# ScalarE issues the mixing weights during step A; table parts, stores and conversion work move later

## The chip, the cores and the metric

One core of a Trainium2 chip. The metric is the device time of one execution of the kernel in microseconds (us), median of the runs. The engines are named as the profile names them: PE (TensorE, matmuls; PEld are its weight loads), DVE (VectorE), ACT (ScalarE), POOL (GpSimd) and SP (SyncE, which here only issues DMAs). ACT and POOL can issue DMAs too; "ACTq", "SPq" mark such instructions in the rows.

## The reference

A Fourier transform along the sequence, a complex mixing of the 256 channels with a soft threshold, the inverse transform, and then a two-layer network with a leaky activation on every token:

```python
def _attn_ref(x, w_r, w_i, b_r, b_i):          # x: (4, 3008, 256)
    X = np.fft.rfft(x, axis=1)
    Yr = Xr @ w_r - Xi @ w_i + b_r
    Yi = Xr @ w_i + Xi @ w_r + b_i
    Yr = np.sign(Yr) * np.maximum(np.abs(Yr) - 0.01, 0.0)   # and Yi alike
    return np.fft.irfft(Yr + 1j * Yi, n=x.shape[1], axis=1)

def _moe_ref(x, w_in, w_out, alpha):           # x: (12032, 256), d_ff 2048
    h = x @ w_in
    g = np.maximum(h, 0.0) + alpha * np.minimum(h, 0.0)
    return g @ w_out
```

## The kernel before

**Staging.** The transform of length 3008 = 47 x 64 is done in steps for each of the four batch elements. Step A (`a_load`, `a_mm`, `a_evac`) multiplies groups of rows by a small table (`lf_s`); batch 0 keeps its result in SBUF (`a0_s`), batch 1 stores it to DRAM (`ad`) from tiles called `ast`. Step B (`b_load` or `b_half`, `b_mm`) gathers that result transposed into tiles `bt` and multiplies it by the table `rb_s`; the mixing (`m_mm`, `m_evac`) multiplies by `w_r` and `w_i` and applies the threshold; step C (`c_mm`, `c_evac`) multiplies by the table `cf_s` and stores to DRAM (`zd`); step D (`d_load`, `d_step`) loads that back (`zt`) and turns it into tokens. After it the network's two layers run over chunks of tokens (`l1_step` and `l2_step` over the first twelve, `s_l1` and `s_l2` over the rest), with the other batch elements' steps worked in between. This main part takes over nine tenths of the time.

**The start.** Everything that this change touches lies before the main part. Steps A of batch 0 and the first four groups of batch 1 come first (loop over `seq`), then a loop over `t` from 0 to 12: turn `t` runs `b_mm(t)`, `m_evac(t-2)`, `m_mm(t-1)`, `c_mm(t-3)` and `c_evac(t-4)`. Behind the loop a list `TAIL` ends step C, then has the ten remaining early groups of step A of batch 1 (entries `f`, function `a_fill`), and step D's first two loads (entry `d`). Then step D and the first layer begin.

**The conversion.** Beside these turns the network's weights, 16 raw pieces of 512 KB, are loaded (`conv_load`, line L265) and split into a high and a low part for the matmuls. A piece's operations are cut into packets, four to a piece, in which the end of one piece is worked together with the beginning of the next. `pump(n)` works the next n packets; the list `PT` says how many in each turn. On ACT the packets show as L278 (first look at a raw piece; it waits for that piece's load), L287 and L288; on DVE as L279, L280, L289, L293, L296; on POOL as L290, L297. When `pump` starts a piece it also lets `conv_fetch` issue loads so that two raw pieces are on their way. Pieces 0 to 7 can be loaded from the start; 8 to 15 only after turn 10 has set `conv_m[1] = FT`.

**What sets the order.** The order on each engine is the order of this code (`manual_schedule`). Each engine works its list strictly in order, and an instruction whose data or buffer isn't there holds all behind it. PSUM tiles of steps A to C come from a pool of three (`ps_f`, tag `f`): a matmul group of step A needs the tile that the group three before it has been evacuated from. The mixing's PSUM tiles come from a pool of two. DMAs of SP and ACT share eight completion counters, and a DMA waits until the earlier one on its counter has landed. The tile `Yc` has one buffer; the fourth `ast` tile of batch 1 lives in it first, so the first `m_evac` (ACT, L514) waits until the store of that tile has landed.

Of the kernel before, what the change touches and what calls it, by code (L numbers as in the profile page):

```python
# [21 lines left out]
NSLOT = 24  # L22
# [74 lines left out]
def fft_mix_moe(ctx, tc, x, w_r, w_i, b_r, b_i, w_in, w_out, alpha, la, rb, lc, rd, lf, cf, sel, out):  # L97
    nc = tc.nc
# [51 lines left out]
    rb_s = const.tile([128, NSLOT, 128], F32, tag="rb", name="rb_s")  # L150
# [57 lines left out]

    mix_w = []

    def load_mix(*tags):
        for w, tag in zip((w_r, w_i), tags):
            t = work.tile([128, CT, C], F32, tag=tag, name="wm_f", bufs=1 if tag[1] in "tc" else None)
            nc.sync.dma_start(out=t, in_=w.rearrange("(k p) f -> p k f", p=128))
            mix_w.append(t)

    def load_rb(n0, n1, at=0):
        nc.sync.dma_start(out=rb_s[:, n0:n1], in_=rb[:, n0 + at:n1 + at])

    def load_cf(n0, n1):  # L220
        nc.gpsimd.dma_start(out=cf_s[:, n0:n1], in_=cf[:, n0:n1])
# [35 lines left out]
    def conv_load():  # L257

        m, i = divmod(conv_m[0], 2)
        conv_m[0] += 1  # L260
        k = conv_m[0] % 3
        raw = cw_s[:, NSLOT + 8 * k:NSLOT + 8 * k + 8].rearrange("p (k n) f -> p k (n f)", k=2)
        raw = raw.rearrange("p k (n w) -> p k n w", w=2)
        src = w_out.bitcast(U32)[256 * m:256 * m + 256] if i else w_in.bitcast(U32)[:, 512 * m:512 * m + 512]
        nc.sync.dma_start(out=raw.rearrange("p k n w -> p k (n w)"), in_=src.rearrange("(k p) f -> p k f", p=128))  # L265
        conv_raw.append((raw, m, i))

    def conv_first(raw, m, i):
        h, m = divmod(m, FH // 2)
        hi, lo = (wo_h[h][:, 2 * m:2 * m + 2, w] if i else wi_h[h][:, w, :, 256 * m:256 * m + 256] for w in range(2))  # L270
        shape = list(hi.shape)
        wh, wl = raw[:, :, :, 1], raw.bitcast(U16)[:, :, :, 1]
        tags = [conv_tags[k][(conv_m[0] + len(conv_raw)) % 2] for k in ("v1", "ex", "lf")]
        v1, ex, lf = (work.tile(shape, t, tag=tag, name="conv", bufs=3 if tag == "bt" else None)
                      for t, tag in zip((U32, U32, F32), tags))
        conv_old.append((wh, wl, v1, ex, lf, hi, lo))
        return [
            lambda: A.activation(out=f(v1), in_=f(wh), func=AF.Abs),  # L278
            lambda: V.tensor_scalar(out=f(v1), in0=f(v1), scalar1=LEAST, scalar2=MOST, op0=ALU.max, op1=ALU.min),  # L279
            lambda: V.tensor_scalar(out=v1, in0=v1, scalar1=0x07FFFFFF, scalar2=3,  # L280
                                    op0=ALU.bitwise_and, op1=ALU.logical_shift_left)]

    def conv_second(wh, wl, v1, ex, lf, hi, lo):
        es = V if ES[(conv_m[0] - 3 + len(conv_raw)) % len(ES)] else G

        def parts():
            A.activation(out=hi, in_=f(v1), func=AF.Copy)  # L287
            A.activation(out=lf, in_=wl, func=AF.Copy, scale=2.0 ** -36)  # L288
            V.tensor_scalar(out=ex, in0=v1, scalar1=0xFF800000, scalar2=None, op0=ALU.bitwise_and)  # L289
            G.tensor_tensor(out=lf, in0=lf, in1=f(ex), op=ALU.mult)  # L290

        return [
            lambda: V.scalar_tensor_tensor(out=v1, in0=wh, scalar=0xC0000000, in1=v1,  # L293
                                           op0=ALU.bitwise_and, op1=ALU.bitwise_or),
            parts,
            lambda: es.tensor_tensor(out=f(v1), in0=f(v1), in1=f(hi), op=ALU.subtract),  # L296
            lambda: G.tensor_tensor(out=lo, in0=f(v1), in1=lf, op=ALU.add)]  # L297
# [12 lines left out]
    def conv_fetch():  # L310
        assert not conv_ops
        while len(conv_raw) < 2 and conv_m[0] < conv_m[1]:
            conv_load()

    def pump(n):

        while n > 0:
            if not conv_ops:
                conv_fetch()
                second = conv_second(*conv_old.pop()) if conv_old else []  # L320
                first = conv_first(*conv_raw.pop(0)) if conv_raw else []
                first, second = ([(op,) for op in ops] for ops in (first, second))
                if first and second:
                    conv_ops.extend([second[0] + first[0], first[1], second[1], second[2] + second[3] + first[2]])
                else:
                    conv_ops.extend(first + second)
                if not conv_ops:
                    return
            for op in conv_ops.pop(0):
                op()  # L330
            n -= 1
# [67 lines left out]
    def a_evac(b, g):  # L399
        ps = pa.pop((b, g))  # L400
        if b == 0:
            st = a0_s[:, g]
        else:
            tag = A1_TAGS[g] if b == 1 and g < len(A1_TAGS) else "zst"
            st = work.tile([NQ, 2, C], F32, tag=tag, name="ast", bufs={"bt": 3, "zst": 3, "Yt": 1, "Yc": 1}.get(tag))
        if b == 0 and g % 2:
            V.tensor_copy(out=st, in_=ps)
        else:
            A.activation(out=st, in_=ps, func=AF.Copy)
        if b:  # L410
            stores.append((ad[b][:, 2 * g:2 * g + 2], st))
# [179 lines left out]
    def d_load(b, g):  # L591
        assert len(zdone) >= NPAIR * (b + 1) and not any(o.tensor is zd[b][:].tensor for o, i in stores)
        t = work.tile([NQ, CH, C], F32, tag="zt", name="zt")
        nc.sync.dma_start(out=t, in_=zd[b][:, CH * g:CH * (g + 1)])
        zt[b, g] = t
# [388 lines left out]
    NG = R // 2  # L984
    EARLY = 4
    FILL = 14
    C0 = 2
    PT = [0, 1, 3, 3, 3, 3, 3, 3, 4, 4, 4, 4]
    TAIL = [['me', 1], ['ce', 3], ['cm', 2], ['cm', 1], ['ce', 2], ['ce', 1], ['d'], ['f', 4], ['e'], ['f', 6]]
    WARM = 6  # L990
    A1_TAGS = ("zst", "zst", "Yt", "Yc", "bt", "bt", "bt", "Xh", "Xl", "Xh", "Xl", "zst", "zst", "Yc")
# [3 lines left out]
    def keep_warm(n):  # L995
        ps = ps_f.tile([128, 512], F32, tag="f", name="ps_idle")
        for _ in range(n):
            PE.matmul(ps[:, 0:128], idle, idle, start=True, stop=True)

    with tc.manual_schedule():  # L1000
# [6 lines left out]
            a_load(0, g)  # L1007
        for g in range(EARLY // 2):
            a_load(1, g)
        load_rb(0, 4, NSLOT)  # L1010
        load_mix("Yh", "Yh")
        conv_tags.update(v1=("yh", "yl"), ex=("xh", "xh"), lf=("xl", "xl"))
        seq = [(0, g) for g in range(NG)] + [(1, g) for g in range(EARLY)]

        for n, (b, g) in enumerate(seq):
            a_mm(b, g)
            if n >= 1:
                a_evac(*seq[n - 1])
            if n == NG // 2:
                b_half(0, 0)  # L1020
                b_half(1, 0)
            if n == NG:
                b_half(0, 1)
                b_half(1, 1)
                b_load(0, 2)
                load_rb(4, 12)
                for _ in range(C0):
                    conv_load()
                bias_parts()
# [5 lines left out]
        def run(fn, q, *args):  # L1035
            if 0 <= q < NPAIR:
                fn(0, q, *args)
# [10 lines left out]
        for t in range(NPAIR + 1):  # L1048
            if t == 1:
                keep_warm(8)  # L1050
            run(b_mm, t)
            run(b_load, t + 3)
            run(c_evac, t - 4)
            run(b_evac, t)
            run(m_evac, t - 2)
            run(m_mm, t - 1, ps_h)
            run(b_evac2, t)
            run(c_mm, t - 3)
            if t < NPAIR:
                pump(PT[min(t, len(PT) - 1)])  # L1060
            if t in (2, 5):
                load_rb(2 * t + 8, 2 * t + 14)
            if t < 8 and t % 2 == 0:
                load_cf(3 * t, 3 * t + 6)
            if t == 1:
                put()
            if t == 6:
                load_tables()
            if 5 <= t < 10:
                a_load(1, t - 3)  # L1070
            if t == NPAIR - 1:
                load_rb(0, 4)
            if t == 10:
                half(1)
                conv_m[1] = FT
        for op, *args in TAIL:
            if op == "f":
                a_fill(*args)
            elif op == "d":

                drain()
                d_load(0, 0)
                d_load(0, 1)
                conv_fetch()
                conv_m[1] = conv_m[0]
                hold.extend(conv_raw)
                conv_raw.clear()
            elif op == "e":
                flush()
            elif op == "p":  # L1090
                pump(*args)
            else:
                {"me": m_evac, "cm": c_mm, "ce": c_evac}[op](0, NPAIR - args[0])
# [126 lines left out]
        for k in range(len(spairs) + SLAG):  # L1220
# [9 lines left out]
            if k >= SLAG:  # L1230
                n, t = spairs[k - SLAG]
# [43 lines left out]
```

## Time and profile before

| | |
|---|---|
| median of 3 runs | 1354.2 us (1352.36 to 1355.0) |
| the profiled execution's own time | 1353.91 us |
| its span, first to last instruction | 1352.1 us |
| granted TensorE clock, mean | 1.000 |
| busy share of the span | PE 99%, PEld 92%, DVE 77%, ACT 56%, POOL 27% |
| chain of waits that ended last, share of the span | PE 89%, DMA 3%, DVE 2%, ACT 2%, issue 2% |
| mean busy share of the DMA engines in the first seven of 40 slices | 0.9, 0.9, 0.7, 0.4, 0.2, 0.2, 0.3 |

A busy PE isn't a PE at its peak: the ends of matmuls are modelled, and a matmul that starts late behind a wait shows the wait in brackets. In the timelines a row reads: start, duration, engine, line, operation, out<-in, shape, how many; in brackets the idle time of that engine just before and what ended it. Start to start of equal matmuls is the better measure of PE's pace. A queue's row gives packets, MB and its share of the time of the 16 DMA engines; a row of DMA issues gives how many, KB each and the median time to landing. A row of a merged group covers its members from the first start to the last end.

### The profile page before, as it was taken

Reading aid. Unit: us, or ns where it says so; the run is one execution under the profiler, and the core shown is the slowest. Engines: PE = TensorE matmul, PEld = TensorE weight load, DVE = VectorE, ACT = ScalarE, POOL = GpSimd, SP = SyncE. Lnnn points to the kernel's source line nnn. Section 1 sums busy time; section 2 is a strip of 40 time slices with the busy share of each in tenths; the row PEclk is TensorE's granted clock in tenths of the full one; section 3 lists DMA queues with packets and bytes.
Section 4 is the critical chain, followed back from the end, with each engine's and each line's share of the span. In section 5 each row is a group of like instructions: output and inputs, shape, how many; then the busy total and the mean of one; then the engine's idle time right before and its main releaser. Section 6 shows DMA issues by size and latency. Waiting matters only on the chain.

```text
span 1352.1 us, 25037 instructions
## 1 busy us (share of the span) xinstructions
PE 1334.2 (99%) x9144; PEld 1248.6 (92%) x9144; DVE 1034.8 (77%) x1940; ACT 761.3 (56%) x1526; POOL 371.7 (27%) x398
## 2 busy tenths in 40 slices
PE   8989999999999999999999999999999999999998
PEld 4969999999999999999999999999999999999998
DVE  3766866776777777776768888888888888888885
ACT  3556655665565655545556555555565555555653
POOL 3754642221322232222212211212112111211122
PEclk9999999999999999999999999999999999999999
DMA  9974223342334312111110110111011101110001
GB/s 226 246 203 152 88 95 98 104 135 86 98 97 129 98 64 82 48 55 48 36 36 1 40 29 1 40 28 28 3 38 28 29 5 36 29 28 7 23 17 28
DMA packets 88278, 89.91 MB, mean 66 GB/s; under 512 B 42157, under 2 KB 70544, under 8 KB 88155
## 3 DMA queue, kind: packets, MB, share of 16 engines
q1 hardware_dynamic: 80116, 77.55, 20.2%
q0 software_dynamic: 4912, 7.76, 2.2%
q10 hardware_dynamic: 3127, 3.01, 0.7%
q8 instruction: 72, 1.18, 0.4%
q14 instruction: 51, 0.42, 0.1%
HBM read 50.76 MB, written 34.34 MB: 63 GB/s over the span
## 4 chain that ended last, share of the span: by engine, by line
PE 89%; DMA 3%; DVE 2%; ACT 2%; issue 2%; POOL 0%; SPq 0%; ACTq 0%; DVEq 0%; POOLq 0%
PE ps_h L804 24%; PE ps_h L699 13%; PE ps_m L501 6%; PE ps_o L905 6%; PE ps_o L906 6%; PE ps_o L904 6%; PE ps_d L630 4%; PE ps_o L738 3%; PE ps_o L737 3%; PE ps_o L736 3%; PE ps_b L438 2%; PE o_last L737 1%; PE o_last L738 1%; PE o_last L904 1%; PE o_last L736 1%
## 5 line engine op out<-in xcount | busy, mean ns | idle before, releaser
L804 PE MATMUL ps_h<-yh,w 128*128 128x512 f32 (+1 forms) x960 | 315.6, 389 | 0.0
L843 POOL TENSOR_TENSOR l<-t,h 128x512 fp32r<-128x512 f32 x98 | 127.1, 1297 | 496.5 <-ACT h L841 455.7
L804 PEld LDWEIGHTS ps_h<-yh,w 128*128 128x128 f32 x960 | 180.0, 188 | 33.2
L808 DVE SCALAR_TENSOR_TENSOR sq<-sq,beta_s,ps_h 128x512 f32<-128x512 f32 (+1 forms) x240 | 167.8, 732 | 54.5 <-ACT sq L807 53.7
L699 PE MATMUL ps_h<-yh,w 128*128 128x384 f32 (+1 forms) x704 | 207.0, 337 | 1.3 <-DVE q L706 1.3
L804 PE MATMUL ps_h<-yl,w 128*128 128x512 f32 (+1 forms) x480 | 186.2, 388 | 0.0
L706 DVE SCALAR_TENSOR_TENSOR q<-q,beta_s,ps_h 128x384 f32<-128x384 f32 (+1 forms) x192 | 115.1, 600 | 91.8 <-ACT q L705 90.9
L710 ACT ACTIVATE gh<-q 128x384 fp32r<-128x384 f32 (+1 forms) x192 | 99.1, 516 | 148.6 <-DVE q L706 145.6
L711 POOL TENSOR_TENSOR gl<-q,gh 128x384 fp32r<-128x384 f32 (+1 forms) x90 | 96.8, 1076 | 275.9 <-ACT gh L710 266.4
L823 ACT ACTIVATE dh<-sq 128x768 fp32r<-128x768 f32 x112 | 94.8, 846 | 117.8 <-DVE sq L808 75.9
L807 ACT ACTIVATE sq<-ps_h 128x512 f32<-128x512 f32 (+1 forms) x240 | 133.2, 586 | 26.8 <-PE ps_h L804 25.5
L699 PEld LDWEIGHTS ps_h<-yh,w 128*128 128x128 f32 x704 | 129.3, 189 | 4.4 <-DVE q L706 1.2
L705 ACT ACTIVATE q<-ps_h 128x384 f32<-128x384 f32 (+1 forms) x192 | 91.9, 479 | 61.3 <-PE ps_h L699 60.5
L841 ACT ACTIVATE h<-t 128x512 fp32r<-128x512 f32 x98 | 62.0, 633 | 105.5 <-DVE t L839 103.2
L699 PE MATMUL ps_h<-yl,w 128*128 128x384 f32 (+1 forms) x352 | 116.5, 331 | 0.0
L738 PE MATMUL ps_o<-w,gl 128*128 128x256 f32 x384 | 108.0, 281 | 0.6 <-POOL gl L711 0.6
L737 PE MATMUL ps_o<-w,gh 128*128 128x256 f32 x384 | 107.8, 281 | 0.0
L736 PE MATMUL ps_o<-w,gh 128*128 128x256 f32 x384 | 107.7, 280 | 0.0
L804 PEld LDWEIGHTS ps_h<-yl,w 128*128 128x128 f32 x480 | 90.5, 189 | 13.6
L838 DVE TENSOR_TENSOR dl<-sq,dh 128x768 fp32r<-128x768 f32 x98 | 93.4, 953 | 3.8 <-ACT dh L823 3.7
L906 PE MATMUL ps_o<-l,sw_a 128*128 128x256 f32 x294 | 82.0, 279 | 0.0
L904 PE MATMUL ps_o<-h,sw_a 128*128 128x256 f32 x294 | 81.9, 279 | 0.0
(215 smaller groups left out, 3610.4 us busy)
## 6 DMA issues: line engine op xcount, KB each, us to landing
zt<-zd SPq DMA_DIRECT2D x32, 384.0 KB
zd<-zst SPq DMA_DIRECT2D x37, 256.0 KB
ad<-ast SPq DMA_DIRECT2D x48, 192.0 KB
bt<-ad SPq DMA_DIRECT2D x72, 128.0 KB
xt<-in_x SPq DMA_DIRECT2D x21, 320.0 KB
out<-oT SPq DMA_DIRECT2D x152, 32.0 KB
cw_s<-in_moe_w_in SPq DMA_DIRECT2D x8, 512.0 KB
cw_s<-in_moe_w_out SPq DMA_DIRECT2D x8, 512.0 KB
```

What stands on the lines that cost most here:

```text
L699: PE.matmul(ps, wi_h[m // FH][:, w, ct, 128 * (m % FH):128 * (m % FH) + 128], a[:, ct, 0:n], start=(k == 0), stop=(k == 3 * CT - 1))
L706: V.scalar_tensor_tensor(out=q, in0=q, scalar=beta_s[:, m:m + 1], in1=ps, op0=ALU.mult, op1=ALU.add)
L710: A.activation(out=hi, in_=q, func=AF.Copy)
L736: PE.matmul(a, hi[:, t], w[:, 0], start=(i, k) in first, stop=False)
L737: PE.matmul(a, hi[:, t], w[:, 1], start=False, stop=False)
L738: PE.matmul(a, lo[:, t], w[:, 0], start=False, stop=(i, k) in last)
L804: PE.matmul(ps, wi_h[m // FH][:, w, ct, 128 * (m % FH):128 * (m % FH) + 128], a[:, ct, 0:w1], start=(k == 0), stop=(k == 3 * CT - 1))
L807: A.activation(out=q[:, j], in_=ps, func=AF.Relu, scale=-1.0)
L808: V.scalar_tensor_tensor(out=q[:, j], in0=q[:, j], scalar=beta_s[:, m:m + 1], in1=ps, op0=ALU.mult, op1=ALU.add)
L843: G.tensor_tensor(out=l24, in0=t24, in1=f(h24), op=ALU.subtract)
L904: PE.matmul(o, wh, gh, start=first, stop=False)
L906: PE.matmul(o, wh, gl, start=False, stop=last)
```

## The change

Five edits:

- The three transfers of the mixing stage (`rb_s` table parts 0 to 3, `w_r`, `w_i`) are issued by ACT in the eighth turn of step A's loop (between ACT's fourth and fifth evacuation), not by SP behind all of step A's row loads.
- `C0`: one raw piece, not two, is loaded ahead of the loop over `t`; the next is then issued by `pump` in turn 1.
- `put()`, the four stores of batch 1's `ast` tiles, is called in turn 3, not turn 1; the table part `rb` 12 to 17 in turn 3, not 2; the parts of `cf` in turns 0, 3, 6, 8, not 0, 2, 4, 6.
- `PT`: turns 8 to 11 work three packets each, not four (31 in all before `TAIL`, 35 before).
- The four packets left over are worked in `TAIL`'s entry `d`, behind the issue of step D's two loads.

```diff
-    def load_mix(*tags):
+    def load_mix(*tags, queue=nc.sync):
...
-            nc.sync.dma_start(out=t, in_=w.rearrange("(k p) f -> p k f", p=128))
+            queue.dma_start(out=t, in_=w.rearrange("(k p) f -> p k f", p=128))
...
-    def load_rb(n0, n1, at=0):
-        nc.sync.dma_start(out=rb_s[:, n0:n1], in_=rb[:, n0 + at:n1 + at])
+    def load_rb(n0, n1, at=0, queue=nc.sync):
+        queue.dma_start(out=rb_s[:, n0:n1], in_=rb[:, n0 + at:n1 + at])
...
-    C0 = 2
-    PT = [0, 1, 3, 3, 3, 3, 3, 3, 4, 4, 4, 4]
+    C0 = 1
+    PT = [0, 1, 3, 3, 3, 3, 3, 3, 3, 3, 3, 3]
...
-        load_rb(0, 4, NSLOT)
-        load_mix("Yh", "Yh")
...
+            if n == 7:
+                load_rb(0, 4, NSLOT, nc.scalar)
+                load_mix("Yh", "Yh", queue=nc.scalar)
...
-            if t in (2, 5):
-                load_rb(2 * t + 8, 2 * t + 14)
-            if t < 8 and t % 2 == 0:
-                load_cf(3 * t, 3 * t + 6)
-            if t == 1:
+            if t in (3, 5):
+                load_rb(3 * t + 3, 3 * t + 9)
+            if t in (0, 3, 6, 8):
+                load_cf((t + 1) // 3 * 6, (t + 1) // 3 * 6 + 6)
+            if t == 3:
                 put()
...
                 d_load(0, 0)
                 d_load(0, 1)
+                pump(4)
                 conv_fetch()
```

**ACT, from the end of step C to step D** (L580 and L584: evacuation and store of step C; L409: evacuation of a group of step A). Before:

```order
L514 ACTIVATE Yc<-ps_m,lam_s 128x512 x2
L580 ACTIVATE zst<-ps_c 128x512
L584 DMA zd_437<-zst 128x2x256
L580 ACTIVATE zst<-ps_c 128x512
L584 DMA zd_437<-zst 128x2x256
L409 ACTIVATE ast<-ps_a 96x512 x4
L287 ACTIVATE w_911<-conv 128x2x256
L288 ACTIVATE conv<-cw_s 128x512
L409 ACTIVATE ast<-ps_a 96x512 x6
```

Now:

```order
L514 ACTIVATE Yc<-ps_m,lam_s 128x512 x2
L580 ACTIVATE zst<-ps_c 128x512
L584 DMA zd_431<-zst 128x2x256
L580 ACTIVATE zst<-ps_c 128x512
L584 DMA zd_431<-zst 128x2x256
L278 ACTIVATE conv<-cw_s 128x512
L287 ACTIVATE w_258<-conv 128x2x256
L288 ACTIVATE conv<-cw_s 128x512
L409 ACTIVATE ast<-ps_a 96x512 x4
L287 ACTIVATE w_903<-conv 128x2x256
L288 ACTIVATE conv<-cw_s 128x512
L409 ACTIVATE ast<-ps_a 96x512 x6
```

Three conversion operations now stand ahead of the evacuations of step A's ten groups; the first of them, L278, reads raw piece 8.

**SP, the same place** (L265: raw pieces; L218: the `rb` table; L584: a store of step C; L594: step D's loads). Before, where the first two L265 are raw pieces 8 and 9 and the third is piece 10:

```order
L265 DMA cw_s<-in_moe_w_in 128x2x512
L265 DMA cw_s<-in_moe_w_out 128x2x512
L218 DMA rb_s<-tab_rb 128x512
L584 DMA zd_437<-zst 128x2x256
L594 DMA zt<-zd_437 96x1024 x2
L265 DMA cw_s<-in_moe_w_in 128x2x512
L594 DMA zt<-zd_437 96x1024
```

Now, where the three L265 are pieces 8, 9 and 10:

```order
L218 DMA rb_s<-tab_rb 128x512
L584 DMA zd_431<-zst 128x2x256
L594 DMA zt<-zd_431 96x1024 x2
L265 DMA cw_s<-in_moe_w_in 128x2x512
L265 DMA cw_s<-in_moe_w_out 128x2x512
L265 DMA cw_s<-in_moe_w_in 128x2x512
L594 DMA zt<-zd_431 96x1024
```

Raw pieces 8 and 9 have moved from ahead of step C's last store to behind step D's first two loads.

**SP, from step A's last loads to the fourth raw piece** (L214: mixing weights; L420: gathers of step A's result; L339: the four `ast` stores). Before:

```order
L218 DMA rb_s<-tab_rb 128x512
L214 DMA wm_f<-in_w_r 128x2x256
L214 DMA wm_f<-in_w_i 128x2x256
L420 DMA bt<-a_83 64x1x256 x4
L218 DMA rb_s<-tab_rb 128x1024
L265 DMA cw_s<-in_moe_w_in 128x2x512
L265 DMA cw_s<-in_moe_w_out 128x2x512
L339 DMA ad_159<-ast 96x512 x4
L265 DMA cw_s<-in_moe_w_in 128x2x512
L218 DMA rb_s<-tab_rb 128x768
L265 DMA cw_s<-in_moe_w_out 128x2x512
```

Now:

```order
L420 DMA bt<-a_83 64x1x256 x4
L218 DMA rb_s<-tab_rb 128x1024
L265 DMA cw_s<-in_moe_w_in 128x2x512
L265 DMA cw_s<-in_moe_w_out 128x2x512
L265 DMA cw_s<-in_moe_w_in 128x2x512
L218 DMA rb_s<-tab_rb 128x768
L339 DMA ad_159<-ast 96x512 x4
L265 DMA cw_s<-in_moe_w_out 128x2x512
```

The first three rows have gone to ACT, and the four stores stand behind a third raw piece and a table part that followed them.

## Rows read from the trace of the kernel before

**Rows 1.** Stretches: busy us (count) of PE, PEld, DVE, ACT, POOL; clock, DMA share, GB/s

```profile
44.82:69.14 24.32, 24.32 (x186) 23.48 (x185) 21.13 (x28) 14.64 (x25) 22.28 (x27) 1.00 0.99 244
69.14:74.50 5.36, 5.09 (x38) 4.74 (x37) 3.88 (x5) 1.69 (x3) 5.02 (x6) 1.00 1.05 215
74.50:81.43 6.93, 5.39 (x39) 4.88 (x37) 4.24 (x7) 3.83 (x7) 2.51 (x3) 1.00 0.89 265
81.43:95.57 14.14, 12.14 (x76) 10.04 (x75) 10.90 (x18) 8.29 (x15) 10.51 (x11) 1.00 0.54 164
```

**Rows 2.** Timeline of PE: step A's ten groups of batch 1, idle matmuls, step D

```profile
95.57 8.76 PE L392 MATMUL ps_a<-xt,lf_s 94*96 94x512 f32 x24
104.16 0.83 PE L998 MATMUL ps_idle<-idle 128*128 128x128 bf16 x12
104.83 2.87 PE L630 MATMUL ps_d<-rd_s,zt 96*128 96x94 f32 x24
```

**Rows 3.** Timeline of ACT over the same stretch

```profile
97.04 1.08 ACT L409 ACTIVATE ast<-ps_a 96x512 f32<-96x512 f32 x2 [0.67 <-PE ps_a L392]
...
99.75 0.62 ACT L287 ACTIVATE w<-conv 128x512 fp32r<-128x512 f32 x1
100.27 0.66 ACT L288 ACTIVATE conv<-cw_s 128x512 f32<-128x512 uint16 x1
100.84 1.59 ACT L409 ACTIVATE ast<-ps_a 96x512 f32<-96x512 f32 x3
```

**Rows 4.** Timeline of SP's queue over the same stretch

```profile
98.54 0.81 SPq L594 DMA_DIRECT2D zt<-zd  x2
99.40 0.42 SPq L265 DMA_DIRECT2D cw_s<-in_moe_w_in  x1
```

**Rows 5.** DMA between 98.5 and 105.0: GB/s in 40 equal slices, and the sum

```profile
GB/s 0 0 0 0 0 0 176 176 0 126 176 277 328 479 429 277 353 303 227 277 252 277 227 265 277 240 252 252 214 239 328 391 403 378 277 164 25 0 0 0
DMA packets 496, 1.31 MB, mean 202 GB/s; under 512 B 48, under 2 KB 48, under 8 KB 496
```

**Rows 6.** Waits of SP's queue, 92 to 112: total us, times, longest

```profile
SPq L594 <- DMA zt<-zd: 2.6, 1, 2.6
```

**Rows 7.** Timeline of PE, turns 10 to 12: first matmul of the mixing

```profile
77.10 0.50 PE L481 MATMUL ps_m<-bias_p,ones 128*128 128x512 f32 x1 [1.54 <-DVE Y L515]
...
82.97 0.50 PE L481 MATMUL ps_m<-bias_p,ones 128*128 128x512 f32 x1 [0.49 <-DVE Y L515]
...
88.32 0.50 PE L481 MATMUL ps_m<-bias_p,ones 128*128 128x512 f32 x1 [0.85 <-DVE Y L515]
```

**Rows 8.** Timeline of ACT in turn 9: raw piece 6

```profile
78.28 0.66 ACT L278 ACTIVATE conv<-cw_s 128x512 f32<-128x512 f32 x1 [1.96 <-DMA cw_s<-in_moe_w_in]
78.85 0.62 ACT L287 ACTIVATE w<-conv 128x512 fp32r<-128x512 f32 x1
```

**Rows 9.** Timelines of SP, PE and ACT in the first turns, by engine

```profile
17.68 0.37 SPq L214 DMA_DIRECT2D wm_f<-in_w_i  x1
...
25.60 0.68 PE L438 MATMUL ps_b<-rb_s,bt 128*128 128x128 f32 x4 [1.12 <-DMA bt<-a]
27.84 0.68 PE L438 MATMUL ps_b<-rb_s,bt 128*128 128x128 f32 x4 [1.57 <-DMA bt<-a]
...
40.81 0.47 PE L481 MATMUL ps_m<-bias_p,ones 128*128 128x512 f32 x1
...
38.11 0.69 ACT L514 ACTIVATE Yc<-ps_m,lam_s 128x512 f32<-128x512 f32 x1 [2.59 <-DMA ad<-ast]
```

**Rows 10.** DMA: POOL's queue and issues, 28 to 34; SP's queue, 26 to 42

```profile
q0 software_dynamic: 42, 0.00, 0.6%
...
bt<-a POOLq DMA_DIRECT2D x4, 128.0 KB, 11.5
...
q1 hardware_dynamic: 1728, 3.43, 71.3%
```

**Rows 11.** Timeline of PE at the start of the kernel: idle matmuls

```profile
1.00 4.02 PE L998 MATMUL ps_idle<-idle 128*128 128x128 bf16 x36 [1.00 <-DVE idle L1001]
```

## The prediction

> **What bounds the kernel now.** I read first the busy shares (PE 99%), then the chain of waits. PE has 89% of the chain, and in the main part nothing changes, so only the start can move the time, and what is lost or won before step D shifts all that follows. Then I read the start by stretches. From 44.8 to 69.1 PE is the bound: 24.32 us for five turns, 4.86 us each, with PE never idle [rows 1]. From 69.1 to 95.6 it is not: PE has gaps, while DVE and POOL do conversion work [rows 1]. In turns 10 to 12 the mixing's first matmul waits 1.54, 0.49 and 0.85 us for the threshold's result [rows 7]; the first follows raw piece 6, for which ACT waited until 78.28 [rows 8]. From 95.57 PE is the bound again: step A's ten groups take 8.76 us, 0.86 each, to 104.3, then idle matmuls, then step D at 104.83 [rows 2]. ACT evacuates those groups at once, the first at 97.04 [rows 3]. Before 44.8 the DMAs are late: step B's first matmuls wait 1.12 and 1.57 us for gathers, and ACT's first threshold waits 2.59 us, to 38.11, for the fourth `ast` store [rows 9].
>
> **The change part by part.** I sum from the end of step C, because that part is the largest.
>
> *Four packets behind step D's loads.* Raw piece 8 was loaded in turn 11. Now its load is issued by the `pump(4)` behind step D's two loads, and ACT's L278, which reads it, stands ahead of all ten evacuations. PE can do three groups of step A, as there are three PSUM tiles; the fourth waits for the first evacuation. So PE waits for this: step C's last store lands, SP issues step D's two loads and then piece 8, piece 8 lands, ACT does three operations and an evacuation. In the trace of before the same three transfers stand in the same order (there the third is piece 10): SP issues the loads at 98.54 and the piece at 99.40 [rows 4]. Their 1.31 MB keep the DMA engines busy until the last full slice, some 104.5 [rows 5]. A transfer's counter rises later than its last byte: SP waited 2.6 us from 99.82, that is to 102.4, for the first of the two loads [rows 6], by whose end some 0.39 MB had been moved, at about 101.1 [rows 5]. So piece 8 lands between 104.5 and 105.8; I take 105.5. Then L278 to L287 takes 0.57 us start to start [rows 8], L287 to L288 0.52 and L288 to the evacuation 0.57 [rows 3], the evacuation some 0.6: PE goes on at 107.8. Seven groups of 0.86 are left, 6.0 us, to 113.8 instead of 104.3: **+9.5 us** (bounds 8.5 and 9.8). The cover is PE's three groups, 2.6 us, which is in the sum. Behind the waiting L278 are all evacuations; behind SP's next instruction, piece 10, which waits for conversion of piece 7, stand the third load of step D and ten stores, which nothing needs before step D is under way.
>
> *Three packets a turn, not four.* With four, turns 8 to 11 have the stretch from 74.5 to 95.57, 21.07 us. At PE's pace it would be two turns of 4.86, one without step B (4.86 less eight matmuls, 4.05) and two last step C's of 0.86: 15.5 us. So 5.6 us are to be had at most. 1.5 of them, the wait ending at 77.10 [rows 7], stay: raw piece 6 is asked for in the same place of SP's list. Of the rest I followed ACT's new list from 78.28 on: L287 and L288 (1.1 us, [rows 3, 8]) no longer stand between L278 and the next threshold, so turn 11's mixing starts when PE is free, not at 82.97, and turn 12's at about 86.7, not at 88.32 [rows 7]; the last threshold then ends step C at some 92.8 instead of 95.6. **-2.8 us** (bounds 0 and -4.1).
>
> *The stores in turn 3.* Nothing on SP's list holds pieces 1 and 2 back, so all the same transfers are issued one after another, as before; one raw piece first changes nothing by itself. But the four stores now stand behind a third raw piece and a table part, 0.92 MB, of the 3.43 MB that SP's queue moves from 26 to 42 [rows 10]: 3.4 to 4.3 us later at 0.27 to 0.21 MB a microsecond [rows 1, 10]. ACT's first threshold waited for the fourth store to 38.11, and the mixing of turn 3, which needs that tile's result, started at 40.81 [rows 9]; DVE's 0.7 us and ACT's 0.7 lie between, so 1.3 us are free, and 2.1 to 3.0 are not. I take the lower end, since a landing may also come ahead of the queue's last byte: **+2.0 us** (bounds 0 and +3).
>
> *Mixing weights from ACT.* SP issued the last of them at 17.68, behind all rows of x [rows 9]. ACT issues them earlier, three issues of some 0.4 in the 1.1 us that it has between evacuations (every second group, 1.72 us, less 0.6). But they use three of the eight counters: SP's last loads of x now wait for their landing, and come later by up to 3 us (0.79 MB at 0.24 a microsecond, [rows 1]). PE had 2.7 us of waiting for gathers between 24.5 and 27.84 [rows 9], and this covers it: 0 (bounds -1.0, as the gathers no longer share the queue with the weights, and +1.5). There is a reason to price it higher. From 28 to 34 POOL's queue got 0.6% of the DMA engines' time, though it issued gathers there, which took 11.5 us to land [rows 10]: SP's transfers went first, so x would go before the weights. The Trainium skill (DMA: Bandwidth & Descriptors, Queues, rings and completion order) says that the engines take turns between queues; by this the weights' 0.79 MB would delay x by up to their own time, and the term would be +1.5. The trace of before bears that out only in part, since these rows show no turns.
>
> *Table parts.* The last part of `cf`, 0.39 MB, moves from turn 6 into turn 8, where the DMA engines are full (share 1.05, [rows 1]) and piece 6 is on its way. At 215 to 265 GB/s it is 1.5 to 1.8 us of their time, part of it before piece 6: **+0.7 us** (0 to +1.3). The others move by a turn ahead of need and cost nothing.
>
> *PE's pace after the wait.* PE stands from about 98.2 to 107.8. No row of before has so long a standstill, and the granted clock reads 1.00, the level of 2.4 GHz, in every stretch that I read [rows 1]. The nearest row is the kernel's beginning, where PE had done nothing: 36 idle matmuls took 4.02 us, 112 ns each [rows 11], where 12 later take 0.67 between their first start and step D, 56 each [rows 2]. That is 2.0 us lost. I take **+2.0 us** (0 if the pace stays, +6.0 if all seven groups run at half). The Trainium skill (TensorE: Matmul & The Clock Gate, Part 1) says that half rate is the state of an idle PE and that work lifts it; that speaks for a loss and against 0.
>
> Sum: 9.5 - 2.8 + 2.0 + 0 + 0.7 + 2.0 = +11.4 us. The sum is made on the profiled execution, 1353.9 us (span 1352.1 and 1.8 around it), 0.3 under the median; on the median of 1354.2 it gives 1365.6.
>
> **The rivals.**
>
> - *The clock stays up.* For it: the granted clock never falls in before. Against: the start's pace. 2.0 less, 1363.6. Chance 0.15.
> - *The early part is free and three packets give all they can.* The stores overtake, and turns 10 to 12 gain 4.1: 11.4 - 2.0 - 1.3 = +8.1, 1362.3. For it: DVE is busy 10.90 of 14.14 us there. Against: ACT's list is the bound at 82.97, not DVE. Chance 0.12.
> - *Half pace for all seven groups.* For it: the start's 36 matmuls all ran so. Against: they were 4.0 us of work, the groups are 6.0 and more. +4.0 more, 1369.6. Chance 0.12.
> - *Piece 8 is there in time (not slower).* If its transfer were not behind step D's loads and landed before about 96.5, ACT's three operations, 1.7 us, would lie beside PE's three groups, and nothing of the 9.5 and of the 2.0 would remain. With the early part free and 4.1 gained the time is 1350.1. The point from which it decides is that landing; each us behind it costs a us. Against: the order puts its issue behind loads that wait for step C's last store. Chance 0.05. Halfway (piece 8 some 4 us late, the gain kept) it ends within 0.2%: 0.05.
> - That the four packets don't stand where the text says is excluded by the order: 31 are worked in the turns, and L278 stands ahead of the evacuations.
>
> **How the numbers follow.** The forecast as summed has 0.51, the rivals 0.15, 0.12, 0.12, 0.05 and 0.05. The likeliest is the forecast, 1365.6. The range leaves out the last two and what lies past the slow-clock case: 1359 (all terms but the first at their better ends give 1358.6) to 1371. A measurement of this kernel can tell about 0.2%, 2.7 us (its three runs spread over 2.6). Faster by more: 0.05; within: 0.05; slower: 0.90.
>
> **What the profile after would show.** Right: ACT idle before an L278 ahead of step A's ten evacuations, ended by the DMA of a raw piece; PE idle 8 to 10 us after three groups; step D some 10 us later; the last step C at 92 to 96 plus what the start lost; the first threshold waiting for an `ast` store until 41 or 42. Wrong: the ten groups in one run of 9 us, or a gap of 3 us only; or the end of step C earlier than 90, which would make the first turns, not the tail, what I misjudged.

## The result and the profile after

The changed kernel takes **1372.5 us** (median; 1370.9 to 1375.1) where the kernel before takes 1354.7 (1352.4 to 1357.6) on the same chip: a ratio of 1.0132, 95% interval 1.0114 to 1.0151, or 17.7 us more. The forecast was 11.4 us more, 1365.6 with a range of 1359 to 1371. So the direction was right and the size too small by 6.3 us.

The two profiled executions differ by 19.1 us in span (1371.2 and 1352.1), and nearly all of it is there when step D begins: at 123.61 instead of 104.83, 18.8 us later. The rest, from step D's first matmul to the end of the span, takes 1247.2 to 1247.6 us in the traces of all kernels of this study but one (1250.3, where step D begins at half pace). So four marks ahead of that say where the time went: the mixing's first matmul in turn 1, step B's first in turn 4, the first of step A's ten groups, and step D's first.

| mark | before | after | lost since the mark ahead |
|---|---|---|---|
| mixing of turn 1 (first L481) | 30.62 | 35.51 | +4.89 (from the beginning) |
| step B of turn 4 (L438) | 44.82 | 48.91 | -0.80 (+4.09 in all) |
| step A's ten groups (L392) | 95.57 | 98.52 | -1.14 (+2.95 in all) |
| step D (L630) | 104.83 | 123.61 | +15.83 (+18.78 in all) |

**The tail**, PE's timeline of the changed kernel from step A's first groups of batch 1 to step D (start, duration, line, count, idle time before and what ended it; to be laid beside [rows 2]):

```profile
98.52 2.74 PE L392 MATMUL ps_a<-xt,lf_s 94*96 94x512 f32 x6
110.39 12.26 PE L392 MATMUL ps_a<-xt,lf_s 94*96 94x512 f32 x18 [9.13 <-ACT ast L409]
122.44 1.33 PE L998 MATMUL ps_idle<-idle 128*128 128x128 bf16 x12
123.61 2.87 PE L630 MATMUL ps_d<-rd_s,zt 96*128 96x94 f32 x24
```

The one run of 8.76 us is now in two pieces, with 9.13 us of idle PE between them. ACT's and SP's timelines of the same kernel name the reason (beside [rows 3, 4]):

```profile
108.11 0.66 ACT L278 ACTIVATE conv<-cw_s 128x512 f32<-128x512 f32 x1 [8.80 <-DMA cw_s<-in_moe_w_in]
108.67 0.62 ACT L287 ACTIVATE w<-conv 128x512 fp32r<-128x512 f32 x1
109.19 0.67 ACT L288 ACTIVATE conv<-cw_s 128x512 f32<-128x512 uint16 x1
109.76 1.54 ACT L409 ACTIVATE ast<-ps_a 96x512 f32<-96x512 f32 x3
...
114.15 0.59 ACT L409 ACTIVATE ast<-ps_a 96x512 f32<-96x512 f32 x1
115.86 0.59 ACT L409 ACTIVATE ast<-ps_a 96x512 f32<-96x512 f32 x1 [1.11 <-PE ps_a L392]
...
101.61 0.80 SPq L594 DMA_DIRECT2D zt<-zd  x2
102.51 0.39 SPq L265 DMA_DIRECT2D cw_s<-in_moe_w_in  x1
```

ACT waits 8.80 us in front of L278 for raw piece 8, which SP asked for at 102.51, behind step D's loads, and which landed 5.6 us later. The evacuations (L409) stand behind it. From 114.15 on they come every 1.71 us, and ACT waits 1.11 us for PE ahead of each of the last five: PE is the bound there, at half its former pace of 0.86 a group. The stretches show the clock (busy us and count of PE, PEld, DVE, ACT, POOL; granted clock; DMA share; GB/s):

```profile
20.00:25.00 5.00, 3.89 (x5) 1.21 (x6) 1.12 (x4) 0.59 (x1) 0.00 (x0) 0.61 0.74 137
25.00:30.00 5.00, 5.00 (x7) 1.70 (x6) 0.78 (x2) 1.39 (x3) 1.35 (x2) 0.50 0.43 90
...
105.00:110.00 5.00, 0.00 (x0) 0.00 (x0) 1.10 (x3) 1.89 (x4) 0.07 (x1) 0.50 0.73 243
...
115.00:120.00 5.00, 5.00 (x8) 1.86 (x8) 0.99 (x1) 1.78 (x3) 2.22 (x2) 0.50 0.00 0
120.00:125.00 5.00, 5.00 (x32) 4.01 (x30) 0.00 (x0) 1.46 (x3) 0.00 (x0) 0.65 0.00 0
```

The granted clock is at 0.50, the level of 1.2 GHz, both in the standstill (from 103; PE had stopped at 101.25) and while PE works through the seven groups. It was also at 0.50 from 25 to 30, in **the start**, where the profile of the kernel before reads 1.00 in every stretch. There PE's timeline and ACT's queue read (beside [rows 9]):

```profile
20.60 3.25 PE L392 MATMUL ps_a<-x,lf_s 94*96 94x512 f32 x4 [2.34 <-DMA x<-in_x]
24.36 7.11 PE L392 MATMUL ps_a<-xt,lf_s 94*96 94x512 f32 x8 [0.51 <-DMA xt<-in_x]
43.70 1.16 PE L438 MATMUL ps_b<-rb_s,bt 128*128 128x128 f32 x8 [0.92 <-DMA bt<-a]
...
12.53 0.66 ACTq L214 DMA_DIRECT2D wm_f<-in_w_r  x1
13.22 0.48 ACTq L214 DMA_DIRECT2D wm_f<-in_w_i  x1
...
43.27 0.69 ACT L514 ACTIVATE Yc<-ps_m,lam_s 128x512 f32<-128x512 f32 x1 [2.87 <-DMA ad<-ast]
```

PE stood 2.34 us for `x`, and the last groups of step A then ran at half pace: step A ended at 31.26. In the kernel before it had ended at 23.97, where the idle matmuls begin:

```profile
20.54 3.60 PE L392 MATMUL ps_a<-xt,lf_s 94*96 94x512 f32 x8
23.97 0.50 PE L998 MATMUL ps_idle<-idle 128*128 128x128 bf16 x6
```

The waits of SP's queue between 8 and 26 us (line, what it waited for: total, times, longest) say why `x` was late:

```profile
SPq L363 <- DMA wm_f<-in_w_r: 2.1, 1, 2.1
SPq L363 <- DMA rb_s<-tab_rb: 1.7, 1, 1.7
SPq L363 <- DMA wm_f<-in_w_i: 1.1, 1, 1.1
```

SP held back its last loads of `x` 4.9 us in all until ACT's three transfers had landed. The kernel before has no such row; its `x` loads wait only for one another, 4.7 us, in the change 5.6 and these 4.9.

### The profile page after: what moved, and what is told of

It is laid out like the page before. It is cut to its first block, busy times and chain, and to the rows that moved or that the text cites. A ratio compares the mean times of both kernels' runs of the same rounds, so it can differ in the third digit from the quotient of the medians.

```text
span 1371.2 us, 25037 instructions
## 1 busy us (share of the span) xinstructions
PE 1346.0 (98%) x9144; PEld 1253.0 (91%) x9144; DVE 1039.3 (76%) x1940; ACT 761.2 (56%) x1526; POOL 373.3 (27%) x398
## 3 DMA queue, kind: packets, MB, share of 16 engines
q8 instruction: 72, 1.18, 0.4%
## 4 chain that ended last, share of the span: by engine, by line
PE 89%; DMA 4%; DVE 2%; issue 2%; ACT 2%; POOL 0%; SPq 0%; ACTq 0%; DVEq 0%; POOLq 0%
PE ps_h L804 24%; PE ps_h L699 13%; PE ps_m L501 6%; PE ps_o L905 6%; PE ps_o L906 6%; PE ps_o L904 5%; PE ps_d L630 4%; PE ps_o L738 3%; PE ps_o L737 3%; PE ps_o L736 3%; PE ps_b L438 2%; PE ps_a L392 2%; PE o_last L737 1%; PE o_last L738 1%; PE o_last L904 1%
## 5 line engine op out<-in xcount | busy, mean ns | idle before, releaser
L737 PE MATMUL ps_o<-w,gh 128*128 128x256 f32 x384 | 107.8, 281 | 0.0
```

The source lines that it names most:

```text
L737: PE.matmul(a, hi[:, t], w[:, 1], start=False, stop=False)
```

## Experiments

Each ratio is against runs of the kernel before on the same chip, whose median was 1353.3 to 1354.0 there.

**One part alone: the mixing weights** (kernel before, plus)

```diff
-        load_rb(0, 4, NSLOT)
-        load_mix("Yh", "Yh")
...
+            if n == 7:
+                load_rb(0, 4, NSLOT, nc.scalar)
+                load_mix("Yh", "Yh", queue=nc.scalar)
```

> The kernel before with the first edit alone: ACT issues the rb part and the mixing weights in the eighth turn of step A's loop. Theory A (the start's loss is the weights': they delay the last rows of x, PE stands in step A, its clock falls to 1.2 GHz and step A's last groups run at half pace): 3 to 5 us slower than before, PE waiting over 2 us on x near 18 us and a granted clock of 0.5 between 22 and 31 us, step C's last matmul 3 to 5 us later. Theory B (the start's loss is the four stores', which hold ACT's first threshold): 0, within 1 us of before, and the clock at 1.00 throughout.

1358.6 us, ratio 1.0043 (1.0026 to 1.0060), 5.3 us more. PE's timeline shows the same start as in the change:

```profile
21.26 3.53 PE L392 MATMUL ps_a<-x,lf_s 94*96 94x512 f32 x4 [3.00 <-DMA x<-in_x]
24.59 7.03 PE L392 MATMUL ps_a<-xt,lf_s 94*96 94x512 f32 x8
```

The weights do cost: the term priced at 0, with +1.5 as its upper bound, was wrong.

**One part alone: the tail**

```diff
-    PT = [0, 1, 3, 3, 3, 3, 3, 3, 4, 4, 4, 4]
+    PT = [0, 1, 3, 3, 3, 3, 3, 3, 3, 3, 3, 3]
...
                 d_load(0, 1)
+                pump(4)
                 conv_fetch()
```

> The kernel before with the packets alone: three a turn in turns 8 to 11, four behind step D's first loads. Theory A (PE stands for raw piece 8 and then runs its last seven step A groups at half pace; turns 10 to 12 give back about 1): 14 to 15 us slower, a PE gap of 9 us after three groups and seven groups of 1.7 us. Theory B (the seven groups were slow in the changed kernel because the clock had fallen already at the start): 8 to 9 us slower, the gap the same, the groups 0.86 us each.

1370.0 us, ratio 1.0126 (1.0108 to 1.0144), 16.7 us more, with the rows of the change's tail, PE's above ACT's:

```profile
108.79 12.26 PE L392 MATMUL ps_a<-xt,lf_s 94*96 94x512 f32 x18 [9.17 <-ACT ast L409]
...
106.51 0.66 ACT L278 ACTIVATE conv<-cw_s 128x512 f32<-128x512 f32 x1 [8.83 <-DMA cw_s<-in_moe_w_in]
```

**One part alone: one raw piece, stores and table parts later** (the diff's lines on `C0`, `put`, `load_rb(3 * t + 3, ...)` and `load_cf`)

> The kernel before with one raw piece first, the four stores in turn 3 and the table parts later. Theory A (the stores matter only as far as the start isn't late for another reason): 1 to 3 us slower by the time step C begins, ACT's first threshold waiting for a store until 41 or 42 us, and 0 to 3 us at the end. Theory B (nothing of it is on the path, as DMAs carry the same bytes): within 0.7 us of before, and the first matmul of turn 3's mixing at 40.8 as before.

1357.0 us, ratio 1.0030 (1.0021 to 1.0039), 3.7 us more. ACT's first threshold waits longer for the fourth store, and the mixing of turn 3 waits with it:

```profile
41.46 0.69 ACT L514 ACTIVATE Yc<-ps_m,lam_s 128x512 f32<-128x512 f32 x1 [4.87 <-DMA ad<-ast]
...
42.93 0.50 PE L481 MATMUL ps_m<-bias_p,ones 128*128 128x512 f32 x1 [3.02 <-DVE Y L515]
```

To tell the stores from the raw piece, each was also changed alone: `put()` at t == 3 instead of 1, and `C0 = 1` instead of 2.

> The kernel before with only the ad stores moved from turn 1 to turn 3. ScalarE's L514 waited 2.59 us for such a store in the kernel before and 4.87 us in the run with all of the stores' and tables' edits, which took 3.7 us more. Theory A (that later store is the whole of the 3.7 us): 3 to 4.5 us more than before, with L514 waiting 4 to 5 us. Theory B (the one raw piece or the table parts make it): at most 1 us more.

> The kernel before with only one raw piece loaded ahead of the turns instead of two. Theory A (the stores make the loss; one raw piece less ahead of the ad stores lets these and step B's reloads land sooner): the same as before or up to 2 us less. Theory B (the second piece comes late and the conversion in turns 1 to 3 waits for it): 1 to 4 us more.

The late stores alone: 1359.0 us, ratio 1.0037 (1.0024 to 1.0050), 5.0 more; L514 waited 3.91 us. One raw piece alone: 1354.8, ratio 1.0003 (0.9994 to 1.0012), nothing. So it is the stores; the intervals of the two kernels with late stores overlap between 3.2 and 5.3 us. The table parts were not run alone. The price rests on the medians: in the trace of the late stores alone 3.8 us of the lateness are there at turn 1 already (its first L481 is at 34.41), ahead of L514's wait, so this trace doesn't show that wait as the whole cause.

**The clock in the tail** (the change, plus 150 idle matmuls between step A's third and fourth group, into a PSUM tile that nothing reads)

> The changed kernel with 150 idle matmuls (some 8.4 us of PE's time, into a PSUM tile that nobody reads) between the third and the fourth of the ten step A groups behind step C, where PE stands for raw piece 8. Theory A (the wait for the piece costs 9 us and the pace after it another 6.5): the wait stays, the seven groups go back to 0.86 us each, the granted clock stays 1.00 there, and the time is 5 to 7 us under the changed kernel, about 1366. Theory B (the groups are slow because evacuations or DMA traffic slow them): no change, 1372.

The median is 1369.4, ratio 1.0127 (1.0091 to 1.0164), but the runs lie far apart: 1364.6, 1366.4, 1372.4 and 1375.7, with mean granted clocks of 0.996, 0.992, 0.993 and 0.988. The profiled one is the first; PE's timeline:

```profile
98.22 8.54 PE L998 MATMUL ps_busy<-idle 128*128 128x128 bf16 x150
108.75 6.26 PE L392 MATMUL ps_a<-xt,lf_s 94*96 94x512 f32 x18 [1.98 <-ACT ast L409]
```

and a stretch of it:

```profile
105.00:110.00 5.00, 3.02 (x35) 2.16 (x33) 2.73 (x4) 3.31 (x7) 1.71 (x2) 1.00 0.31 96
```

There the clock stays at 1.00 and the seven groups take 6.26 us instead of 12.26, although the fourth group comes 13.1 us after the first (11.87 in the change). From the first group to step D (115.52) it is 19.9 us instead of 25.1. So in this trace the half pace is gone when PE's standstill is filled, while the wait for the piece and the evacuations behind it are as they were. The times show less: the interval holds the change's own ratio, two of the four runs lie under every run of the change (lowest 1370.9), two don't, and why can't be told, as they have no trace. The next kernels, in which the standstill itself is gone, bear the reading out.

**The wait in the tail.** Both kernels here have the four packets behind step D's loads; they only ask for the raw pieces one step earlier, in turn 11, ahead of these loads. The first is the tail's edit alone with this line, the second the whole change with it.

```diff
             if t == NPAIR - 1:
+                conv_fetch()
                 load_rb(0, 4)
```

> The kernel before with the tail's four conversion operations moved behind step D's first loads, as in the change (three in each of the last four turns, four in the tail), but with the loads of the pieces that they convert issued one step earlier, in turn 11, where they don't stand behind step D's loads on SyncE. Theory A (the wait is made by the place of the loads alone: piece 8 is asked for at 102.51 and ScalarE waits for it 8.8 us): with the load out early ScalarE finds the piece landed, the three groups before it are evacuated at once, PE has no standstill over 2 us in the tail, its clock stays at its upper level, the seven groups take some 6 us, and the time is that of the kernel before within 2 us (between 2 us less and 2 us more). Theory B (the four operations cost by themselves in that place, since they stand ahead of seven groups' evacuations on ScalarE): 2 to 6 us more than before, with an idle stretch of 2 to 4 us of PE at the fourth group.

> The changed kernel with one line added: the pieces that the tail's four conversion operations need are loaded in turn 11, ahead of step D's loads. Theory A (the place of the loads costs the whole 15.8 us that the tail lost; the start's 4 us stay): 1356 to 1359 where the kernel before takes 1353.8 and the change 1372.5. Theory B (the four operations, or the later start, keep part of the tail's loss): 1361 or more.

The tail alone with early loads: 1353.5, ratio 0.9999 (0.9989 to 1.0009). The whole change with early loads: 1357.5 (1353.8 to 1363.6), ratio 1.0027 (1.0012 to 1.0041). ACT's and PE's timelines of the first of the two, and PE's of the second:

```profile
95.19 0.68 ACT L278 ACTIVATE conv<-cw_s 128x512 f32<-128x512 f32 x1 [0.44 <-ACT zst L580]
...
97.49 6.26 PE L392 MATMUL ps_a<-xt,lf_s 94*96 94x512 f32 x18 [0.80 <-ACT ast L409]
...
97.96 6.26 PE L392 MATMUL ps_a<-xt,lf_s 94*96 94x512 f32 x18 [0.79 <-ACT ast L409]
```

No DMA ends ACT's wait ahead of L278 any more; the operations cost 0.80 us of PE, no standstill longer than that is left, and the seven groups keep their pace. The place of the loads, not that of the operations, costs the whole tail: one line brings the change's 17.7 us down to 3.5. The kernel with the tail's edit is also the rival of a piece that is there in time. Its mechanism is as described, but the time given for it, 1350.1, took the most from the packets, and 1353.5 shows that this was not gained.

**The clock and the moment in the start.** In the first of the next two, idle matmuls fill PE's standstill in step A (40, 16 and 16, ahead of groups 14, 16 and 18); in the second, ACT issues the weights at n == 11 instead of 7. The rest is the kernel before.

> The kernel before with the mixing weights issued by ScalarE beside step A (as e1_weights, which took 5.3 us more) and with idle matmuls (40, 16 and 16) ahead of three of step A's last groups, where PE stood 3 us for rows in that run, so that PE has work in the standstill. Theory A (two thirds of the loss is PE's pace: step A's last twelve groups took 10.6 us at half speed and would take some 5.6): the clock stays at its upper level from 20 to 35 us, and 1 to 3 us are lost to before instead of 5.3. Theory B (the rows' lateness is the loss, the clock is only its company): no gain from the idle matmuls, 4.5 to 6.5 us more than before.

> The kernel before with the same three transfers on ScalarE's queue, but issued four groups later in step A (some 7 us: about 19 us, after SyncE has issued all its rows' loads, about as late as SyncE issued them in the kernel before). Theory A (what costs is that the two 1 MB weights are in the DMA engines ahead of and between step A's last rows): the rows land as in the kernel before, no standstill of 3 us at 18 to 21 us, and the time is that of before within 1.5 us. Theory B (a second queue takes turns with SyncE's whenever it is used, whatever the moment): the weights then meet the reloads of step B instead, and 3 to 5 us are lost as in e1_weights.

With idle matmuls: 1356.0, ratio 1.0014 (1.0004 to 1.0024), 2.2 us more instead of 5.3, the clock at 1.00 from 15 to 35 us. So by the medians over half of the weights' cost is the clock. One rival stands: the kernel before was not run with these idle matmuls, and most of its own runs have a mean clock under 1.000 (see the end of the next section), so a part of the 3.1 us may be a gain that it would have too. Four groups later: 1354.6, ratio 1.0000 (0.9990 to 1.0010), no loss clear of noise. (The weights are 256 KB each, not the 1 MB of the expectation.) But its rows are not as I had expected, PE's and SP's waits:

```profile
24.54 3.70 PE L392 MATMUL ps_a<-xt,lf_s 94*96 94x512 f32 x4 [2.89 <-DMA xt<-in_x]
...
SPq L420 <- DMA rb_s<-tab_rb: 5.5, 1, 5.5
```

`xt` is late all the same, PE stands 2.89 us, and step A ends at 28.04, 4.1 us late. Next to nothing comes of it because most of step B's reloads then are there: PE waits 0.80 us for them, and the mixing of turn 3 starts at 41.14 instead of 40.81. In the profile of the kernel before PE waits 1.12, 1.57, 0.41, 0.94 and 0.79 us for these reloads, 4.8 us together; about that much lateness the start can swallow.

**Do the parts add up?** The change with the weights back on SP:

> The changed kernel with one part undone: the mixing weights back on SyncE's queue behind step A's rows. Theory A (the parts add up in the time as the traces add: the weights cost the start 4 to 5 us, the rest is the tail): 4 to 6 us less than the changed kernel, 1366.5 to 1368.5 where it takes 1372.5 and the kernel before 1354.7. Theory B (the start's delay is taken up by waits further on, since turns 10 to 12 wait for conversion work either way): at most 2 us less than the changed kernel.

1372.1 us, ratio 1.0134 (1.0117 to 1.0151): no gain. Alone the weights cost 5.3 and the stores' edits 3.7; together they cost 3.5 (the change with early loads). ACT's timeline with the weights undone:

```profile
42.55 0.69 ACT L514 ACTIVATE Yc<-ps_m,lam_s 128x512 f32<-128x512 f32 x1 [4.11 <-DMA ad<-ast]
```

With SP issuing the weights ACT waits 4.11 us for the store, in the change 2.87, and PE's step B of turn 4 comes at 49.71 there and at 48.91 in the change. When PE comes late by the weights, the store has landed meanwhile: the two waits lie beside each other, and taking one away uncovers the other. The profiled execution also kept the low clock for longer than the change did: step D's first matmuls, 2.87 us in the change, ran so (PE's timeline, and a later stretch, in which PE is still without a gap since 108.56):

```profile
121.90 5.38 PE L630 MATMUL ps_d<-rd_s,zt 96*128 96x94 f32 x24
```

```profile
128.00:130.00 2.00, 2.00 (x11) 2.00 (x11) 0.86 (x3) 0.63 (x3) 0.00 (x0) 0.50 1.03 367
```

**A kernel with both moves in a milder place** (weights at n == 11, raw pieces loaded in turn 11, stores and table parts as before):

> The kernel before with both moves in a milder place: the mixing weights on ScalarE's queue four groups later than in the change (about 19 us), and the four conversion operations behind step D's loads with their pieces loaded in turn 11. Each alone took the time of before (1353.5 and 1354.6 beside 1353.8). Theory A (both only keep out of the way, there is nothing to be won in either): within 2 us of before. Theory B (the turns freed of packets and SyncE freed of three issues add up once neither costs): 2 to 5 us less than before.

1354.1, ratio 0.9997 (0.9988 to 1.0006). Neither move shows a gain; no version here beats the kernel before.

## Why the prediction came out too low, point by point

*Four packets behind step D's loads, +9.5: right.* Resumption was forecast 12.2 us after the ten groups' start (107.8 less 95.57); it came 11.87 after. Against groups of 0.86 each, the wait costs 9.3. The early loads show that its cause is the one named. Of the signs listed, the wait and PE's idle time came as said; step D came 18.8 us later, not some 10.

*PE's pace after the wait, +2.0: the step that failed.* It measured 6.5: 12.05 us for seven groups instead of 6.0, and 0.5 on the idle matmuls. That PE would be slow was right; that it would be slow for the first 4 us only was wrong: all seven groups ran at half pace. I had taken the kernel's beginning as the nearest row [rows 11], where 36 idle matmuls at half pace take 4.0 us, and held against the rival of half pace throughout that the groups are longer than that. But step A's groups are other work than a run of idle matmuls: 12.26 us of them passed at 0.50, and the clock rose only behind them (0.50 from 120 to 123, 1.00 from 124; the idle matmuls begin at 122.44). The sentence of the Trainium skill (TensorE: Matmul & The Clock Gate, Part 1), that work lifts the half rate, agrees with the rows only in the end. Nor is it the kind of work alone: with the weights undone the idle matmuls and step D's first ones passed at 0.50 too, and PE worked from 108.56 to 130 before the clock rose. What decides when it rises stays open. No row of before shows step A's groups at the lower level, so the nearest row was one of other work (the granted clock reads 1.00 even there, so that its half pace shows in the matmuls alone), and its 4.0 us were no reason to give the rival 0.12 only. The rival's own sum, 1369.6, lies 2.9 under the result.

*Three packets a turn, -2.8: too good.* The two profiles give -1.14. I had kept the wait that ends at 77.10 fixed, but it fell from 1.54 to 0.67 us, and most of the 1.14 is there. From 78.28 on I had followed ACT's list, and it did get shorter: L278 of raw piece 6 to turn 11's threshold (L514) takes 2.15 us, before 3.23. But the piece itself came later, 2.40 us behind turn 10's mixing instead of 1.18. ACT, PE and DVE of the changed kernel in turns 10 to 12 (beside [rows 7, 8]):

```profile
82.68 0.68 ACT L278 ACTIVATE conv<-cw_s 128x512 f32<-128x512 f32 x1 [3.17 <-DMA cw_s<-in_moe_w_in]
...
84.83 0.68 ACT L514 ACTIVATE Yc<-ps_m,lam_s 128x512 f32<-128x512 f32 x1
...
80.28 0.50 PE L481 MATMUL ps_m<-bias_p,ones 128*128 128x512 f32 x1 [0.67 <-DVE Y L515]
86.29 0.50 PE L481 MATMUL ps_m<-bias_p,ones 128*128 128x512 f32 x1 [0.62 <-DVE Y L515]
91.73 0.50 PE L481 MATMUL ps_m<-bias_p,ones 128*128 128x512 f32 x1 [1.10 <-DVE Y L515]
...
87.89 1.51 DVE L280 TENSOR_SCALAR conv<-conv 128x512 uint32<-128x512 uint32 x1
89.43 1.65 DVE L293 SCALAR_TENSOR_TENSOR conv<-cw_s,conv 128x512 uint32<-128x512 uint32 x1
91.00 0.68 DVE L515 SCALAR_TENSOR_TENSOR Y<-ps_m,Yc 128x512 f32<-128x512 f32 x1
```

and ACT of the kernel before:

```profile
81.51 0.68 ACT L514 ACTIVATE Yc<-ps_m,lam_s 128x512 f32<-128x512 f32 x1
```

From mixing to mixing turns 11 and 12 take 6.01 and 5.44 us; in the kernel before they took 5.87 and 5.35. Turn 11 waits for piece 6, and in turn 12 DVE's two conversion operations, 1.51 and 1.65 us, run without a gap into the threshold's L515: ACT was freed, and the piece and DVE took its place. Nor can the 1.14 be laid to the packets with certainty: the stretch from step B of turn 4 to step A's ten groups takes 48.3 to 51.0 us in the seven traces of kernels with four packets a turn (mean 49.6; the kernel before, 50.75, is near the upper end), and 46.4 to 51.0 in the seven with three (mean 49.2). That the part has next to nothing to give is also what the two kernels with early loads and the stores as before show: in time they equal the kernel before (1353.5 and 1354.1).

*Mixing weights, 0: wrong alone, and hidden in the sum.* Alone they cost 5.3 us. The cover I named, PE's waits for the reloads, is real (4.8 us), but I priced only the lateness of `x` and not that PE's standstill drops the clock: step A's last four groups took 6.9 us from 24.36 to 31.26 instead of 3.4, and so the end of step A came 7.3 us late, more than the cover. The sum by the rule that I had weighed and not taken, +1.5, was nearer, but has no clock in it either. As for the rule (the Trainium skill, DMA: Bandwidth & Descriptors, Queues, rings and completion order: the engines take turns between queues), the trace agrees in so far as both queues were served: in the changed kernel, from 8 to 26 us, ACT's queue had 17.2% of the DMA engines' time beside SP's 60.2%. How much of the lateness of `x` comes of that, and how much of SP's waits of 4.9 us for the shared counters, which I had named with up to 3 us, no run here separates.

*Stores in turn 3, +2.0, and table parts, +0.7.* Alone they cost 3.7 together, near the upper ends of both bounds (4.3), and it is the stores that cost; the mechanism named, ACT's first threshold waiting for a store, is in their trace (4.87 us). In the change the weights' lateness covers part of it. The first threshold came at 43.27, later than the 41 or 42 that I had given as a sign.

So the start, forecast at 0 + 2.0 + 0.7 = 2.7, cost 3.5 (the change with early loads against before; 4.1 by the trace at turn 4): near, but by luck: the weights cost 5.3 alone and not 0, and the parts don't add up as I had summed them. The tail, forecast at 9.5 - 2.8 + 2.0 = 8.7, cost 14.2 by that comparison (17.7 less 3.5), or 14.7 by the trace (15.83 less 1.14): there lies nearly the whole miss, by the trace 4.5 us in the clock and 1.7, as far as two single profiles tell, in the packets.

*What stays open.* One profile is one draw of the start. With the same instructions there, PE waited 1.12 and 1.57 us for the first two reloads in the kernel before, 2.71 and 2.44 with the tail's edit, and the clock then fell as well. The profile of the kernel before is itself the exception: it has a mean granted clock of 1.000, where 70 of the 71 runs of this kernel beside the experiments have 0.995 to 0.999. So "the granted clock never falls in before", said for the first rival, holds for that profile and not for most runs. The change with early loads has runs from 1353.8 to 1363.6, and its profiled one, the fastest, shows step A's end late by 5.6 us and no loss at turn 4 (44.99). I can't say what decides between these. The differences of medians above 2 us whose intervals leave out 1 hold; single rows of the start before 45 us are not a measure of a part of that size.

## What to carry to other kernels

Price an engine's wait twice: once for its length, and once for what a stopped PE does afterwards, at half pace for the whole of the work that follows, until a row shows that just this work lifts the clock. When work is moved behind a queue's other entries, ask where its load is issued, not only where it runs: here one `conv_fetch()` moved ahead takes 14 of 17.7 us away. Costs in a start that waits for DMAs don't add up: two delays lie beside each other, so undo each part in the full change as well as trying it alone.

## What of the hardware was not expected

- PE stayed at 1.2 GHz through 12.26 us of uninterrupted step A groups after 9.13 us of standstill, and in the start through 7.1 us after a standstill of only 2.34 us; the clock fell there some 1 us after PE had gone on (20.60; 1.00 to 21, 0.50 from 22). With the weights undone it stayed there from 108.56 to 130, PE never idle, through step A's groups, idle matmuls, step D's and the first layer's. With idle matmuls in the gap the same groups took 6.26 us at 2.4 GHz, in the one trace of that kernel.
- Transfers issued by ACT held back SP's issues for 4.9 us, where up to 3 had been allowed for. SP waited for their landing; the program has no other tie between them than the shared completion counters. Issued at n == 11, they held back SP's reloads (5.5 us) instead of its rows.
